# Attention scores on four 64x64 blocks of TensorE, a pair of tiles in one PSUM tile, at the start of a round

## The chip, the cores and the metric

The kernel runs on one core of a Trainium2 chip. The metric is the device time of one execution in microseconds. Engines are named as in the profile: PE (TensorE matmuls), PEld (its weight loads), DVE (VectorE), ACT (ScalarE), POOL (GpSimd), SP (the queue that issues most loads). SBUF is the on-chip memory; PSUM is the memory that matmuls write, eight banks of 2 KB in each of 128 partitions.

## What is computed

Attention within chunks of 64 positions, followed by a mixture of experts in which each token goes to one expert:

```python
# q, k, v: (8, 8, 576, 64) float32: batch, head, position, dimension
scores = matmul(q_c, k_c.T) / sqrt(64)        # in each chunk of 64 positions
attn = exp(scores - max(scores)); attn /= sum(attn) + 1e-9
x = matmul(attn, v_c)                         # -> 4608 tokens x 512 (8 heads x 64)
logits = x @ w_gate + modality_bias[modality_id]
e_idx = argmax(logits)                        # one of 8 experts
out[t] = softmax(logits)[e_idx] * (relu(x[t] @ w1[e_idx]) @ w2[e_idx])
```

All of it is float32.

## The kernel before

**Tiles.** The 4608 tokens are 36 tiles of 128 rows: two chunks of 64 positions (c = 0, 1), with all eight heads. For each tile six steps follow each other:

- `scores(t)`: 16 matmuls of 64x64x64, one for each head and chunk. Chunk c has its 64 dimensions on partitions 64c to 64c+63 of the `qk` tile, and its scores go to the same partitions of a PSUM bank `sp`. So the matmuls use two blocks of the 128x128 array by turns: rows 0-63 with columns 0-63, and rows 64-127 with columns 64-127. DVE then takes the maximum of each row of 64 (`mx`, L245) and subtracts it (`ex`, L247), 512 elements a partition each.
- `exps(t)`: the exponential on ACT (L252), and on POOL the first half of the sum (`sr`, L253). `sums(t)` on DVE finishes the sum and takes its reciprocal `ris`, which is applied later.
- `transposes(t)`: four 128x128 transposes of `ex` on PE into a bank `ap` (L264), copied by ACT to `at` (L266).
- `values(t)`: 16 matmuls of 64x64x64 on the two diagonal blocks into a bank `xp` (L278), copied by ACT to `xt` (L281).
- `rows(t)`: four matmuls over the whole array (L290), by the identity and the gate's weights, into `yb[t % 2]`: token rows (128 columns a head pair) and gate logits (16). DVE scales the rows by `ris` into `xr` (L292).
- `put(t)`: ACT copies the logits to `lp` (L302), then issues the DMA of `xr` to DRAM from its own queue (L303).

**Order.** The program is scheduled by hand: every engine runs its instructions in the order in which the code issues them. From tile 2 on, one pass of the main loop (a *round* here, a = 2, 4, ... 34) has two tiles: transposes of a; rows, sums and put of a-2, then of a-1; transposes of a+1; scores of a+2 and a+3; values of a and a+1, with the exps of a+2 ahead and those of a+3 behind. Tiles 0 and 1 go through two single-tile steps. Ahead of the loop stand scores of tiles 0 and 1 and some empty matmuls (`busy`). At the end of every tile `advance()` issues pieces of the routing (`route`, `early_table`, `late_hots`), and `plan` issues gathers, weight loads and weight splits for the last 14 tiles; these add DVE, ACT and POOL work from about a = 14 on.

**Loads.** SP issues `qk` (512 KB a tile, four buffers) right behind the scores that free the buffer, and `v` (256 KB, six buffers) behind the transposes of the round.

**PSUM.** Tag "s" has two banks (`sp`, later `hp` of the experts, and `rp`, `lt`, two of the splits), tag "t" two (`ap`, `xp`, two of the splits, `rp` of the last group, `ll`), `yb` four. A tile of a tag waits until the tile two earlier under that tag has been read.

**Experts.** `split(k)` transposes the first gathered rows (`tp`, L747) and splits them into a high part on ACT (L748) and a low part on DVE (L749). `slot(s)` runs one expert on up to 384 rows; its first layer is `first()` with `hp` (L802), its second L815 into `yb`. The first slot begins as soon as the last tiles are through. Thirteen slots follow each other, with 1248 matmuls of the first layer and 888 of the second.

Of the kernel before, what the change touches and what calls it, by code (L numbers as in the profile page):

```python
# [8 lines left out]
F32 = mybir.dt.float32  # L9
# [4 lines left out]
ALU = mybir.AluOpType  # L14
AX = mybir.AxisListType
# [80 lines left out]
def attention_moe(ctx: ExitStack, tc: tile.TileContext, qkv, mod, cst, bias, wcat, wfst, out):  # L96
# [69 lines left out]

    yb = [ps.tile([P, 2, 512], F32, name=f"yb{i}", bufs=1) for i in range(2)]

    def busy(n):
# [65 lines left out]

    def scores(t):
        b = st[t]["qk"]
        sp = ps.tile([P, H, 64], F32, tag="s", name="sp")
        for h in range(H):
            hs = slice(h * 64, h * 64 + 64)  # L240
            for c in range(2):
                cs_ = slice(c * 64, c * 64 + 64)
                PE.matmul(sp[cs_, h, :], b[cs_, 0, hs], b[cs_, 1, hs], start=True, stop=True)  # L243
        mx = wk.tile([P, H], F32, name="mx", bufs=3)
        V.reduce_max(mx, sp, axis=AX.X)  # L245
        ex = wk.tile([P, H, 64], F32, name="ex", bufs=4)
        V.tensor_tensor(ex, sp, mx.unsqueeze(2).to_broadcast([P, H, 64]), ALU.subtract)  # L247
        st[t]["ex"] = ex

# [71 lines left out]
    def route(g):  # L321
# [69 lines left out]
        ready.add(("ranks", g))  # L391
        rp = ps.tile([P, 2, 32, E], F32, tag="s" if g < NEG else "t", name="rp")
        PE.matmul(rp[:, 0, 0:n], ub, oh, start=True, stop=True)
# [78 lines left out]
    def late_whats(b0, b1):  # L472

        n = b1 - b0
        eq = wk.tile([P, H, 64], F32, name="ex", bufs=4).rearrange("p a b -> p (a b)")
        eq = eq.bitcast(BF16)[:, 0:NT * n].rearrange("p (t b) -> p t b", b=n)
        for a in range(0, NT, NT // 2):
            tp = slice(a, a + NT // 2)
            V.tensor_tensor(eq[:, tp], blkl[:, tp].unsqueeze(2).to_broadcast([P, NT // 2, n]),
                            late_to[0][:, b0:b1].unsqueeze(1).to_broadcast([P, NT // 2, n]), ALU.is_equal)  # L480
            yield
        whats.clear()
        for c in range(NT // PART):
            tp = slice(c * PART, (c + 1) * PART)
            w = wk.tile([P, DM], F32, name="v", bufs=NV).bitcast(BF16)[:, 0:PART * n * 5]
            V.tensor_tensor(
                w.rearrange("p (t b c) -> p t b c", t=PART, c=5),
                eq[:, tp].unsqueeze(3).to_broadcast([P, PART, n, 5]),
                parts[:, tp].unsqueeze(2).to_broadcast([P, PART, n, 5]), ALU.mult)
            whats.append(w.rearrange("p (t m) -> p t m", t=PART))  # L490
            for _ in range(3):
                yield
# [3 lines left out]
    def late_lists(b0, b1):  # L496

        n = b1 - b0
        assert len(whats) == NT // PART and len(late_hot) == NT
        lt = ps.tile([P, n, 5], F32, tag="t", name="ll")  # L500
        for t in range(NT):
# [15 lines left out]
    def early_table(blk, pf, oh, fm):  # L517
# [41 lines left out]
        assert "hot" in ready  # L559
        lt = ps.tile([P, NBLK, 5], F32, tag="s", name="lt")  # L560
        for t in range(n0):
# [178 lines left out]

    def split(k, tag="t"):

        hi, lo = xring[0]
        tp = ps.tile([P, 512], F32, tag=tag, name="tp")[:, 0:SLOT]
        for t in range(NTT):
# [48 lines left out]
    def first(x, w, f, n):  # L794
        hi, lo = x
        whi, wlo = w
        hp = ps.tile([P, 512], F32, tag="s", name="hp")[:, 0:n]
        m = 0
# [101 lines left out]

    scores(0)
    load_qk(NB)
    exps(0)
    late_consts()
    scores(1)
    load_qk(NB + 1)
    busy(BUSY)

    for a, n in [(0, 1), (1, 1)] + [(t, 2) for t in range(2, NT, 2)]:
        hold = transposes(a)  # L910
        if a > 1:
            for t in (a - 2, a - 1):
                rows(t)
                sums(t + 2)
                put(t)
            load_v(a + 2, hold)
            load_v(a + 3, transposes(a + 1))
            for g, (t0, m) in enumerate(GROUPS):
                if t0 + m == a:
                    jobs.append(route(g))  # L920
        else:
            if not a:
                exps(1)
            sums(a)
        small = [t for t in (range(a + 2, a + 4) if a > 1 else (a + 2,)) if t < NT]
        for t in small:
            scores(t)
            load_qk(t + NB)
        if n == 2 and small:
            exps(a + 2)  # L930
        for t in range(a, a + n):
            values(t)
            if small and (n == 1 or t > a):
                exps(small[-1])
            advance()
            plan(t - NT)
            if t >= NT - 2:
                split(t - NT + 2, "s")
        if a == 2:
            prepare()  # L940
# [29 lines left out]
def _pack(inputs):  # L970
# [5 lines left out]
    q, k, v = (chunks(np.asarray(inputs[n])) for n in ("q", "k", "v"))  # L976
    qt = q.transpose(0, 1, 4, 2, 3).reshape(NT, 2, 64, DM)
    kt = k.transpose(0, 1, 4, 2, 3).reshape(NT, 2, 64, DM)
    vv = v.reshape(NT, 2, NP, 2, 64, D).transpose(0, 3, 4, 2, 1, 5).reshape(NT, 2, 64, DM)
    qkv = np.stack([qt, kt, vv], axis=3).reshape(NT, P, 3, DM)  # L980

# [48 lines left out]
```

## Time and profile before

| | us |
|---|---|
| median of 3 runs | 563.91 (561.99 to 564.23) |
| the profiled execution's own time | 564.37 |
| its span in the profile | 562.6 |
| ACT busy | 244.8 |
| POOL busy | 185.0 |
| scores, matmuls (L243) | 38.4 |
| values, matmuls (L278) | 38.5 |

The attention stage covers about the first 137 us; after it the experts' matmuls fill PE to the end. A row of a group gives line, engine, operation, output <- input with shapes, count, busy time and mean ns of one, and behind the last bar the idle time just before and what ended it. A row of the timeline gives start and duration in us and merges equal instructions (x64). A row of a table by stretch gives the stretch, its length, and for each engine busy time and number of records, then the granted clock, the DMA share and GB/s. Matmul ends are modelled by the profiler.

### The profile page before, as it was taken

The numbers are of one execution on the slowest core, as the hardware profiler recorded it, in microseconds if no ns is written. First come the engines' busy times: TensorE is split into PE (matmuls) and PEld (weight loads), VectorE is DVE, ScalarE is ACT, GpSimd is POOL, SyncE is SP. The second block draws the span as 40 slices with busy tenths as digits, with TensorE's granted clock in tenths as the row PEclk, the third lists the DMA queues.
The fourth block names the chain that finished last, engine by engine and source line by source line (L and its number), as shares of the span: only waits on it lengthen the run. The fifth ranks groups of instructions, "written<-read, shape, count | busy, mean of one in ns | idle before, by whom it ended". The sixth has DMA issues, their size and how long they took to land.

```text
span 562.6 us, 12421 instructions
## 1 busy us (share of the span) xinstructions
PE 551.2 (98%) x4950; PEld 501.2 (89%) x4950; DVE 366.4 (65%) x645; ACT 244.8 (44%) x422; POOL 185.0 (33%) x244
## 2 busy tenths in 40 slices
PE   8999999999999999999999999999999999999995
PEld 6999898999998899999898999899899898998994
DVE  4777689788899955655656565565655656556751
ACT  3455555556444333443434434433434434435541
POOL 3322446766699933050220404013040200302011
PEclk9999999999999999999999999999999999999998
DMA  9989989899787469677574966748587673756510
GB/s 329 323 296 309 298 291 296 279 338 313 249 284 223 174 224 317 202 233 224 172 269 150 315 210 190 259 127 276 193 248 219 196 243 121 247 188 215 179 38 26
DMA packets 52754, 130.54 MB, mean 232 GB/s; under 512 B 5198, under 2 KB 22734, under 8 KB 46288
## 3 DMA queue, kind: packets, MB, share of 16 engines
q1 hardware_dynamic: 40864, 100.68, 54.9%
q0 software_dynamic: 5920, 18.88, 8.8%
q10 hardware_dynamic: 5904, 10.11, 4.9%
q8 instruction: 41, 0.67, 0.5%
q14 instruction: 25, 0.20, 0.1%
HBM read 102.12 MB, written 28.05 MB: 231 GB/s over the span
## 4 chain that ended last, share of the span: by engine, by line
issue 49%; PE 32%; POOL 9%; DVE 5%; DMA 2%; ACT 1%; POOLq 0%; ACTq 0%; DVEq 0%
PE hp L802 8%; PE yb L815 7%; PE yb L290 5%; PE sp L243 5%; POOL xg L707 5%; PE xp L278 4%; POOL out L827 3%; PE ap L264 2%; DMA qk<-in_qkv 2%; DVE wl L779 1%; PE yb L171 1%; POOL xq L432 1%; DVE ex L247 0%; DVE mx L245 0%; PE ll L502 0%
## 5 line engine op out<-in xcount | busy, mean ns | idle before, releaser
L779 DVE TENSOR_TENSOR wl<-raw,wh 128x1024 fp32r<-128x1024 f32 (+1 forms) x106 | 128.8, 1216 | 34.9 <-ACT wh L775 34.9
L805 ACT ACTIVATE hh<-hp 128x384 fp32r<-128x384 f32 (+1 forms) x104 | 49.3, 474 | 219.2 <-PE hp L802 218.9
L802 PE MATMUL hp<-xh,wh 128*128 128x384 f32 (+1 forms) x416 | 137.1, 330 | 0.0
L802 PE MATMUL hp<-xh,wl 128*128 128x384 f32 (+1 forms) x416 | 136.8, 329 | 0.0
L802 PE MATMUL hp<-xl,wh 128*128 128x384 f32 (+1 forms) x416 | 136.5, 328 | 0.2 <-DVE xl L739 0.2
L806 DVE SCALAR_TENSOR_TENSOR hl<-hp,hh 128x384 fp32r<-128x384 f32 (+1 forms) x104 | 55.6, 534 | 108.4 <-ACT hh L805 108.4
L815 PE MATMUL yb<-wh,hl 128*128 128x512 f32 x296 | 117.2, 396 | 0.0
L815 PE MATMUL yb<-wl,hh 128*128 128x512 f32 x296 | 116.5, 393 | 0.0
L815 PE MATMUL yb<-wh,hh 128*128 128x512 f32 x296 | 116.5, 393 | 0.0
L827 POOL DMA_INDIRECT out<-yo,tkl x28 | 28.0, 1002 | 248.2 <-DVE yo L826 242.7
L775 ACT CAST wh<-raw 128x1024 fp32r<-128x1024 f32 (+1 forms) x106 | 108.5, 1024 | 0.2 <-issue 0.2
L802 PEld LDWEIGHTS hp<-xl,wh 128*128 128x128 f32 x416 | 78.3, 188 | 4.7 <-DVE xl L739 0.7
L802 PEld LDWEIGHTS hp<-xh,wh 128*128 128x128 f32 x416 | 78.4, 188 | 3.8
L802 PEld LDWEIGHTS hp<-xh,wl 128*128 128x128 f32 x416 | 78.2, 188 | 0.0
L815 PEld LDWEIGHTS yb<-wh,hl 128*128 128x128 f32 x296 | 55.6, 188 | 13.4 <-DVE hl L806 0.6
L815 PEld LDWEIGHTS yb<-wh,hh 128*128 128x128 f32 x296 | 56.0, 189 | 9.1 <-ACT hh L805 0.2
L815 PEld LDWEIGHTS yb<-wl,hh 128*128 128x128 f32 x296 | 55.7, 188 | 9.1
L253 POOL TENSOR_TENSOR sr<-ex 128x256 f32<-128x256 f32 x36 | 26.4, 734 | 65.9 <-ACT ex L252 62.8
L278 PE MATMUL xp<-at,v 64*64 64x64 f32 x1152 | 38.5, 219 | 2.3 <-issue 2.2
L243 PEld LDWEIGHTS sp<-qk 64*64 64x64 f32 x1152 | 35.6, 136 | 4.2 <-DVE sm L257 2.0
L278 PEld LDWEIGHTS xp<-at,v 64*64 64x64 f32 x1152 | 36.0, 135 | 3.5 <-issue 2.9
L243 PE MATMUL sp<-qk 64*64 64x64 f32 x1152 | 38.4, 221 | 0.2 <-issue 0.2
(182 smaller groups left out, 573.9 us busy)
## 6 DMA issues: line engine op xcount, KB each, us to landing
raw<-in_wcat SPq DMA_DIRECT2D x48, 1024.0 KB, 6.2
qk<-in_qkv SPq DMA_DIRECT2D x36, 512.0 KB, 5.8
v<-in_qkv SPq DMA_DIRECT2D x36, 256.0 KB, 4.7
xd<-xr ACTq DMA_DIRECT2D x36, 256.0 KB, 4.8
xs<-xg SPq DMA_DIRECT2D x10, 768.0 KB, 7.2
xq<-xs SPq DMA_DIRECT2D x40, 192.0 KB, 3.4
raw<-in_wfst SPq DMA_DIRECT2D x4, 512.0 KB, 4.9
raw<-in_wfst SPq DMA_DIRECT2D x2, 1024.0 KB, 9.6
```

Of the source, the lines that this page charges most:

```text
L243: PE.matmul(sp[cs_, h, :], b[cs_, 0, hs], b[cs_, 1, hs], start=True, stop=True)
L253: G.tensor_tensor(sring[t % 4][:, :, 0:32], ex[:, :, 0:32], ex[:, :, 32:64], ALU.add)
L278: PE.matmul(xp[hs, p, c * 64:c * 64 + 64], v[hs, vs], at[hs, p, c * 64:c * 64 + 64], start=True, stop=True)
L290: PE.matmul(fp[:, p, 0:GWC], xt[:, p, :], gw[:, p, :], start=True, stop=True)
L707: G.indirect_dma_start(xg[:, t, :], None, xd[0:n, :], bass.IndirectOffsetOnAxis(ap=tk[:, t:t + 1], axis=0), bounds_check=n - 1, oob_is_err ...
L775: A.copy(hi, raw)
L779: (G if pool else V).tensor_tensor(lo, raw, hi.bitcast(F32), ALU.subtract)
L802: PE.matmul(hp, a[:, ks], b[:, k, 0:n], start=(m == 0), stop=(m == 3 * NK - 1))
L805: A.activation(hh[:, 0:n], hp, AF.Relu)
L806: V.scalar_tensor_tensor(hl[:, 0:n], hp, 0.0, hh.bitcast(F32)[:, 0:n], ALU.max, ALU.subtract)
L815: PE.matmul(ys[t], a[:, tsl], b[:, DM:2 * DM], start=(f == 0 and i == 0), stop=(f == NF - 1 and i == 2))
L827: w = G.indirect_dma_start(out, bass.IndirectOffsetOnAxis(ap=tk[:, t:t + 1], axis=0), yo, None, bounds_check=N - 1, oob_is_err=False)
```

## The change

The scores of two tiles are computed together. The host lays q and k out so that the two heads of a pair are on the two halves of the partitions, with both chunks beside each other. Each matmul then takes head half r (rows of the array) and chunk c (columns, and output partitions), and all four combinations occur. Half r writes bank r of a new PSUM tile `sb` of two banks, which holds both tiles of the pair. DVE takes maximum and difference of both tiles at once, 1024 elements a partition. `ex` and `mx` become pair tiles with two buffers each (only tiles 0 and 1 are still done singly, the second one in `yb[0]`).

The order of a round changes too: scores of a+2 and a+3 come first, then transposes of a; rows and sums of a-2 and a-1; transposes of a+1; both put; values of a and a+1. Tiles 0 and 1 become a round of the same form. Since `sb` takes the banks of tag "s", the other users of "s" (`hp`, the first group's `rp`, `lt`, two splits) move to tag "t", and `rp` of the last group and the late lists use the banks of `sb`.

```diff
+    sb = ps.tile([P, 2, 512], F32, name="sb", bufs=1)
...
-    def scores(t):
-        b = st[t]["qk"]
-        sp = ps.tile([P, H, 64], F32, tag="s", name="sp")
-        for h in range(H):
-            hs = slice(h * 64, h * 64 + 64)
-            for c in range(2):
-                cs_ = slice(c * 64, c * 64 + 64)
-                PE.matmul(sp[cs_, h, :], b[cs_, 0, hs], b[cs_, 1, hs], start=True, stop=True)
-        mx = wk.tile([P, H], F32, name="mx", bufs=3)
-        V.reduce_max(mx, sp, axis=AX.X)
-        ex = wk.tile([P, H, 64], F32, name="ex", bufs=4)
-        V.tensor_tensor(ex, sp, mx.unsqueeze(2).to_broadcast([P, H, 64]), ALU.subtract)
-        st[t]["ex"] = ex
+    def scores(a, its=(0, 1), to=None):
+
+        to = sb if to is None else to
+        sp = to.rearrange("q r (b k) -> q r b k", k=64)
+        w = slice(its[0] * NP, its[-1] * NP + NP)
+        for i in its:
+            b = st[a + i]["qk"]
+            for p in range(NP):
+                for r, c in ((0, 0), (1, 1), (0, 1), (1, 0)):
+                    h, o = slice(r * 64, r * 64 + 64), slice(c * 64, c * 64 + 64)
+                    ws = slice((2 * p + c) * 64, (2 * p + c) * 64 + 64)
+                    PE.matmul(sp[o, r, i * NP + p], b[h, 0, ws], b[h, 1, ws], start=True, stop=True)
+        if not its[0]:
+            st[a]["pair"] = (wk.tile([P, 2, 2 * NP], F32, name="mx", bufs=2),
+                             wk.tile([P, 2 * NP, 2, 64], F32, name="ex", bufs=2))
+        mx, ex = st[a]["pair"]
+        mx = mx[:, :, w]
+        V.reduce_max(mx, sp[:, :, w], axis=AX.X)
+        V.tensor_tensor(ex[:, w].rearrange("q a r k -> q r a k"), sp[:, :, w],
+                        mx.unsqueeze(3).to_broadcast([P, 2, len(its) * NP, 64]), ALU.subtract)
+        for i in its:
+            st[a + i]["ex"] = ex[:, i * NP:i * NP + NP].rearrange("q p r k -> q (p r) k")
...
-        rp = ps.tile([P, 2, 32, E], F32, tag="s" if g < NEG else "t", name="rp")
+        rp = ps.tile([P, 2, 32, E], F32, tag="t", name="rp") if g < NEG else \
+            sb[:, 0].rearrange("q (a n e) -> q a n e", a=2, e=E)
...
-        lt = ps.tile([P, n, 5], F32, tag="t", name="ll")
+        lt = sb[:, 1, 0:n * 5].rearrange("p (b c) -> p b c", c=5)
...
-        lt = ps.tile([P, NBLK, 5], F32, tag="s", name="lt")
+        lt = ps.tile([P, NBLK, 5], F32, tag="t", name="lt")
...
-        tp = ps.tile([P, 512], F32, tag=tag, name="tp")[:, 0:SLOT]
+        tp = ps.tile([P, 512], F32, tag="t", name="tp")[:, 0:SLOT]
...
-        hp = ps.tile([P, 512], F32, tag="s", name="hp")[:, 0:n]
+        hp = ps.tile([P, 512], F32, tag="t", name="hp")[:, 0:n]
...
-    scores(0)
+    scores(0, (0,))
     load_qk(NB)
     exps(0)
     late_consts()
-    scores(1)
+    scores(0, (1,), yb[0])
     load_qk(NB + 1)
     busy(BUSY)
-    for a, n in [(0, 1), (1, 1)] + [(t, 2) for t in range(2, NT, 2)]:
+    exps(1)
+
+    for a in range(0, NT, 2):
+        if a + 2 < NT:
+            scores(a + 2)
+            for t in (a + 2, a + 3):
+                load_qk(t + NB)
         hold = transposes(a)
-        if a > 1:
+        if a:
             for t in (a - 2, a - 1):
                 rows(t)
                 sums(t + 2)
+        else:
+            sums(0)
+            sums(1)
+        other = transposes(a + 1)
+        if a:
+            for t in (a - 2, a - 1):
                 put(t)
             load_v(a + 2, hold)
-            load_v(a + 3, transposes(a + 1))
+            load_v(a + 3, other)
...
-        small = [t for t in (range(a + 2, a + 4) if a > 1 else (a + 2,)) if t < NT]
-        for t in small:
-            scores(t)
-            load_qk(t + NB)
-        if n == 2 and small:
+        if a + 2 < NT:
             exps(a + 2)
-        for t in range(a, a + n):
+        for t in (a, a + 1):
             values(t)
-            if small and (n == 1 or t > a):
-                exps(small[-1])
+            if t > a and t + 2 < NT:
+                exps(t + 2)
             advance()
             plan(t - NT)
             if t >= NT - 2:
-                split(t - NT + 2, "s")
+                split(t - NT + 2)
```

On PE, one plain round before stood as follows (`ap`: transposes, `yb`: rows, `sp`: scores, `xp`: values):

```order
L264 MATMUL ap<-cs,ex 128x128 x4
L290 MATMUL yb_94<-cs,xt 128x144 x4
L290 MATMUL yb_95<-cs,xt 128x144 x4
L264 MATMUL ap<-cs,ex 128x128 x4
L243 MATMUL sp<-qk 64x64 x32
L278 MATMUL xp<-at,v 64x64 x32
```

The same round after the change:

```order
L248 MATMUL sb<-qk 64x64 x32
L274 MATMUL ap<-cs,ex 128x128 x4
L300 MATMUL yb_94<-cs,xt 128x144 x4
L300 MATMUL yb_95<-cs,xt 128x144 x4
L274 MATMUL ap<-cs,ex 128x128 x4
L288 MATMUL xp<-at,v 64x64 x32
```

The 32 scores matmuls moved from between the second transposes and the values to the head of the round, so the values now follow the transposes directly.

On ACT, one plain round before (`at`, `xt`: copies of transposes and values, `lp` and `xd`: the two put, `ex`: exponentials):

```order
L266 COPY at<-ap 128x512
L302 COPY lp_132<-yb_94 128x64
L303 DMA xd<-xr 128x512
L302 COPY lp_132<-yb_95 128x64
L303 DMA xd<-xr 128x512
L266 COPY at<-ap 128x512
L252 ACTIVATE ex<-ex 128x512
L281 COPY xt<-xp 128x512 x2
L252 ACTIVATE ex<-ex 128x512
```

After the change:

```order
L276 COPY at<-ap 128x512 x2
L312 COPY lp_133<-yb_94 128x64
L313 DMA xd<-xr 128x512
L312 COPY lp_133<-yb_95 128x64
L313 DMA xd<-xr 128x512
L262 ACTIVATE ex<-ex 128x512
L291 COPY xt<-xp 128x512 x2
L262 ACTIVATE ex<-ex 128x512
```

The second `at` copy moved ahead of both put; the rest kept its order, with the put directly ahead of the first exponential.

On DVE, a plain round before (`xr`: scaled rows, `sm` and `ris`: sums, `mx` and `ex`: maximum and difference of the scores):

```order
L292 TENSOR_TENSOR xr<-yb_94,ris 128x4x4x32
L257 TENSOR_REDUCE sm<-sr_137 128x8
L258 RECIPROCAL ris<-sm 128x8
L292 TENSOR_TENSOR xr<-yb_95,ris 128x4x4x32
L257 TENSOR_REDUCE sm<-sr_138 128x8
L258 RECIPROCAL ris<-sm 128x8
L245 TENSOR_REDUCE mx<-sp 128x8
L247 TENSOR_TENSOR ex<-sp,mx 128x512
L245 TENSOR_REDUCE mx<-sp 128x8
L247 TENSOR_TENSOR ex<-sp,mx 128x512
```

After the change:

```order
L254 TENSOR_REDUCE mx<-sb 128x16
L255 TENSOR_TENSOR ex<-sb,mx 128x2x8x64
L302 TENSOR_TENSOR xr<-yb_94,ris 128x4x4x32
L267 TENSOR_REDUCE sm<-sr_138 128x8
L268 RECIPROCAL ris<-sm 128x8
L302 TENSOR_TENSOR xr<-yb_95,ris 128x4x4x32
L267 TENSOR_REDUCE sm<-sr_139 128x8
L268 RECIPROCAL ris<-sm 128x8
```

Four operations on the scores became two, and they moved ahead of the rows' scaling.

More of the change, by code (lines that the diff above doesn't have):

```diff
@@ L474, in late_whats @@
         n = b1 - b0
-        eq = wk.tile([P, H, 64], F32, name="ex", bufs=4).rearrange("p a b -> p (a b)")
+        eq = wk.tile([P, 2 * NP, 2, 64], F32, name="ex", bufs=2).rearrange("p a r b -> p (a r b)")
         eq = eq.bitcast(BF16)[:, 0:NT * n].rearrange("p (t b) -> p t b", b=n)
@@ L739, in part, with split @@
         V.tensor_tensor(l, x, h.bitcast(F32), ALU.subtract)
-    def split(k, tag="t"):
+    def split(k):
         hi, lo = xring[0]
-        tp = ps.tile([P, 512], F32, tag=tag, name="tp")[:, 0:SLOT]
+        tp = ps.tile([P, 512], F32, tag="t", name="tp")[:, 0:SLOT]
         for t in range(NTT):
@@ L920, in attention_moe @@
                     jobs.append(route(g))
[L921 to L924, printed above, removed]
-        small = [t for t in (range(a + 2, a + 4) if a > 1 else (a + 2,)) if t < NT]
-        for t in small:
-            scores(t)
-            load_qk(t + NB)
-        if n == 2 and small:
+        if a + 2 < NT:
             exps(a + 2)
-        for t in range(a, a + n):
+        for t in (a, a + 1):
             values(t)
-            if small and (n == 1 or t > a):
-                exps(small[-1])
+            if t > a and t + 2 < NT:
+                exps(t + 2)
             advance()
@@ L976, in _pack @@
     q, k, v = (chunks(np.asarray(inputs[n])) for n in ("q", "k", "v"))
[L977 to L980, printed above, removed]
+    q, k, v = (a.reshape(NT, 2, NP, 2, 64, D) for a in (q, k, v))
+    qt = q.transpose(0, 3, 5, 2, 1, 4).reshape(NT, P, DM)
+    kt = k.transpose(0, 3, 5, 2, 1, 4).reshape(NT, P, DM)
+    vv = v.transpose(0, 3, 4, 2, 1, 5).reshape(NT, P, DM)
+    qkv = np.stack([qt, kt, vv], axis=2)
     wg = np.asarray(inputs["moe_w_gate"])
```

## The prediction

> **What bounds the kernel now.** I read the page first, then busy times by stretch, then one round of the timeline.
>
> ```profile
> PE 551.2 (98%) x4950; PEld 501.2 (89%) x4950; DVE 366.4 (65%) x645; ACT 244.8 (44%) x422; POOL 185.0 (33%) x244
> ...
> L243 PE MATMUL sp<-qk 64*64 64x64 f32 x1152 | 38.4, 221 | 0.2 <-issue 0.2
> ```
>
> PE is busy for 98% of the span, so time goes where PE's own stream gets shorter, as long as nothing else closes the gap. The change touches the scores (L243), 38.4 us of PE, all of it in the attention stage. That stage is a chain of rounds of two tiles. Seven rounds run from 21.80 to 71.42, and eight more to 129.20:
>
> ```profile
> core 0: us, PE busy (x) PEld busy (x) DVE busy (x) ACT busy (x) POOL busy (x), PEclk, DMA share, GB/s
> 21.80:71.42 49.62, 48.65 (x1066) 46.71 (x1064) 35.47 (x72) 26.08 (x56) 16.55 (x22) 1.00 0.89 297
> 71.42:129.20 57.78, 56.27 (x1234) 53.88 (x1232) 49.67 (x130) 30.77 (x68) 36.79 (x77) 1.00 0.89 301
> ```
>
> PE is without work for only 1.0 of 49.6 and 1.5 of 57.8 us. DVE has 5.07 us a round in the first stretch and 6.21 in the second, where the routing work is added; the clock is full. One plain round, in the timeline (start, duration):
>
> ```profile
> 49.51 0.66 PE L264 MATMUL ap<-cs,ex 128*128 128x128 f32 x4
> 50.00 2.13 PE L290 MATMUL yb<-cs,xt 128*128 128x144 f32 x16
> ...
> 51.24 0.69 DVE L292 TENSOR_TENSOR xr<-yb,ris 128x512 f32<-128x512 f32 x1 [1.68 <-ACT at L266]
> ...
> 51.96 0.60 PE L264 MATMUL ap<-cs,ex 128*128 128x128 f32 x4
> ...
> 52.42 0.68 DVE L292 TENSOR_TENSOR xr<-yb,ris 128x512 f32<-128x512 f32 x1
> ...
> 52.49 2.08 PE L243 MATMUL sp<-qk 64*64 64x64 f32 x64
> ...
> 53.13 0.21 ACT L302 COPY lp<-yb 128x64 f32<-128x64 f32 x1 [0.96 <-DVE xr L292]
> 53.14 0.64 ACTq L303 DMA_DIRECT2D xd<-xr  x1
> ...
> 53.69 0.69 DVE L245 TENSOR_REDUCE mx<-sp 128x8 f32<-128x512 f32 x1
> 53.88 0.58 ACT L266 COPY at<-ap 128x512 f32<-128x512 f32 x1 [0.53 <-PE sp L243]
> ...
> 54.41 2.03 PE L278 MATMUL xp<-at,v 64*64 64x64 f32 x64
> ...
> 55.20 0.63 ACT L252 ACTIVATE ex<-ex 128x512 f32<-128x512 f32 x1 [0.74 <-DVE ex L247]
> 55.73 0.57 ACT L281 COPY xt<-xp 128x512 f32<-128x512 f32 x1
> ...
> 56.37 0.66 PE L264 MATMUL ap<-cs,ex 128*128 128x128 f32 x4
> ```
>
> From start to start PE spends 0.49 (transposes), 1.96 (rows), 0.53 (transposes), 1.92 (scores) and 1.96 (values): 6.86 us, and nothing else fits between.
>
> **The scores: half, or nothing.** Two tiles are 32 matmuls, and the trace has 64 records for them, two passes each. With 0.22 for the last record, 64 start within 1.86 us: 58 ns a matmul, 29 a pass. A pass of the rows streams 144 columns in 1.96/16 = 0.1225 us, 0.85 ns a column, so 64 columns take some 54 ns. Passes that start 29 ns apart therefore already run two at a time, one on each diagonal block, and each block is full. The change keeps 32 matmuls and 64 passes but gives each of four blocks a quarter of them. No row shows two blocks that share rows or columns of the array. The bounds are 32 x 58/2 = 0.93 us (all four overlap) and 1.87 (the added two take turns with the old). How PE runs past a matmul that waits is seen where its instructions ran out within the values (records in flight in each stretch):
>
> ```profile
> 20.42:20.46 0.04, 0.04 (x4) 1.00 0.26 102
> 20.48:20.52 0.04, 0.04 (x2) 1.00 1.13 410
> 20.53:20.57 0.04, 0.04 (x1) 1.00 2.66 563
> 20.59:21.07 0.48, 0.00 (x0) 1.00 0.86 286
> 61.60:61.62 0.02, 0.02 (x8) 1.00 0.55 205
> 61.63:61.67 0.04, 0.04 (x6) 1.00 0.95 359
> 61.69:61.73 0.04, 0.04 (x4) 1.00 1.05 410
> ```
>
> At 61.6 the stock drains in twos, 8, 6, 4. At 20.4 it drains 4, 2, 1, 0: two single passes, some 55 ns apart, a last matmul alone on its block. In the program both passes of a matmul stand together. If passes began strictly in that order, a second pass would pair with the next matmul's first, and one single pass would be left at the end, not two. So PE starts the other block's matmul ahead of a second pass that waits. That speaks for a bookkeeping by block, and I take 0.93; the end 1.87 stays in the range.
>
> [...]
>
> **DVE.** Four operations of 512 elements (0.69 each, 2.76 us) become two of 1024. The nearest row of that size:
>
> ```profile
> L779 DVE TENSOR_TENSOR wl<-raw,wh 128x1024 fp32r<-128x1024 f32 x102 | 125.7, 1233 | 34.9 <-ACT wh L775 34.9
> ```
>
> That is 2 x 1.23 = 2.46, so 0.3 us less a round. But they now stand ahead of the two xr.
>
> **The new order closes part of the gap.** Count from a round's first scores matmul with 0.98 us for the scores. Alone, PE would be at the next round's scores at 6.86 - 0.94 = 5.92 and at its first transposes at 6.90. These wait for the copy xt(a), since xp and ap share two banks. On ACT xt(a) is behind both lp copies, both DMA issues and one exp. The scores' last pass ends at 1.13; the reduce starts at 1.18 (0.05 later, as at 53.69 behind its own tile), xr(a-2) at 1.18 + 2.46 = 3.64, xr(a-1) 1.18 later (51.24 to 52.42) and ends at 5.50; lp at 5.53; lp to the next ACT work is 0.75 (53.13 to 53.88), so exp at 6.28, xt 0.53 later at 6.81, done at 7.38, seen by PE at 7.45. With the first issue's length (0.33 in place of 0.64) it is 7.13. So the transposes wait 0.23 to 0.55, and from them to the following scores PE needs 0.49 + 1.96 + 0.53 + 1.96 = 4.94. Two rounds take 7.29 + 4.94 = 12.2, one **6.1 us**: 0.76 saved, not 0.94. The copy at(a+1), which was covered by the scores, is now covered by values(a): transposes end about 0.6 after their start, the copy takes 0.58, and values(a+1) come 0.53 + 0.98 after that start, 0.3 to spare.
>
> Seven plain rounds give 7 x 0.76 = 5.3 us. In the other eight DVE has 1.14 us a round more. A plain round leaves DVE free for about 1.3 us before the next reduce, but the extra is uneven:
>
> ```profile
> 85.46:92.69 7.23, 7.20 (x153) 6.83 (x153) 6.81 (x22) 3.58 (x8) 4.57 (x13) 1.00 0.85 279
> 100.87:108.00 7.13, 6.94 (x156) 6.63 (x152) 5.21 (x12) 3.75 (x9) 5.43 (x14) 1.00 0.69 238
> 115.47:122.34 6.87, 6.87 (x157) 6.64 (x153) 5.39 (x15) 3.78 (x9) 3.49 (x5) 1.00 1.04 407
> ```
>
> In the first of these it overflows by half a microsecond, in the second not; POOL's 5.43 and the third's 407 GB/s leave little too. I take 0.5 a round, 4.0 us, between 0.3 and 0.65.
>
> **Two edits that cost.** Splits and hp now draw from the two "t" banks, in the order xp(34), tp, xp(35), tp, tp, tp, hp.
>
> ```profile
> 133.65 0.59 ACT L281 COPY xt<-xp 128x512 f32<-128x512 f32 x1
> ...
> 133.81 1.15 PE L278 MATMUL xp<-at,v 64*64 64x64 f32 x32
> ...
> 136.78 0.86 ACT L748 CAST xh<-tp 128x384 fp32r<-128x384 f32 x2 [0.77 <-PE tp L747]
> ...
> 136.83 0.42 PE L802 MATMUL hp<-xh,wh 128*128 128x384 f32 x1
> ...
> 137.31 1.01 DVE L749 TENSOR_TENSOR xl<-tp,xh 128x384 fp32r<-128x384 f32 x2
> ```
>
> The last values now wait for the copy at 133.65 to end (134.24, not 133.81: 0.45). The first hp waits until DVE has read the third tp, half of 1.01 after 137.31: 137.8 and not 136.83, 1.0. The tp in between wait some 0.3. Sum 1.8 us; nothing hides it, as PE has no other work there. It could be 1 if DVE gets there earlier.
>
> At the start the second pair's scores move ahead of the first transposes and need the fourth qk, which tile 3 used at 11.87 before:
>
> ```profile
> 6.69 8.12 SPq L116 DMA_DIRECT2D qk<-in_qkv  x4
> 8.41 0.66 PE L264 MATMUL ap<-cs,ex 128*128 128x128 f32 x4 [0.28 <-ACT ex L252]
> 11.87 1.15 PE L243 MATMUL sp<-qk 64*64 64x64 f32 x32
> ```
> ```profile
> SPq L116 <- DMA qk<-in_qkv: 3.1, 1, 3.1
> ```
> ```profile
> qk<-in_qkv SPq DMA_DIRECT2D x12, 512.0 KB, 5.4
> ```
>
> After the issue at 6.69 SP waited 3.1 us for the landing of that load, to about 10.1, and then issued the sixth. So the first transposes slip from 8.41 to some 10.8; copy and two values bring PE to 14.2, where the third pair needs the sixth qk (10.2 + 5.4 at the latest, so 14.8 to 15.6); its transposes follow at 15.3 to 16.1 and the next round's 4.94 + 0.98 later, at 21.2 to 22.0, where they were at 21.80. I take 0, within half a microsecond either way. SP's later loads keep two rounds' lead for qk and one for v. The other tile moves (rp, lt, late lists) go to banks that nobody holds then; I cost them at nothing, under 0.3 each if one waits.
>
> **Sum**, against the profiled execution (span 562.6, time 564.37): -5.3 - 4.0 + 1.8 + 0 = -7.5, so 556.9. That execution lies 0.46 above the median of 563.91, so the forecast is **556.4** beside the median. Its own bounds: 0.94 and 0.65 a round with a tail of 1 give 553; 0.6 and 0.3 with the full tail give 560.
>
> **Rivals.**
> - *The added blocks overlap only partly, or the rounds close on transfers.* At 1.4 us a pair PE's round is 6.39: 0.47 x 7 + 0.35 x 8 - 1.8 = 4.3 saved, 560. A round moves 297 GB/s x 7.09 us = 2.1 MB, which in 6.1 us is 345 GB/s. The row with 407 speaks against a hard stop, the share of 0.89 at 297 for later loads and for more time lost where instructions run out. 558 to 563.
> - *The added blocks take turns* (strict order, or one queue for each half of the rows). Rounds stay at 6.86, and tail and start are paid: 564 + 1.8 + 0.3, about 566. The 54 ns that a block's pass needs anyway allow it; the drain speaks against strict order, not against a queue by rows.
> - *Slower: a weight load no longer hides when the block changes within the same rows.* Then each matmul pays one pass more on its half of the rows, 3 x 58 in place of 2 x 58, and 16 a half take 2.8 us in place of 1.87: 17 rounds x 0.93 + 1.8 give 581. It shows as a loss once a matmul costs over 60 ns, since the tail's 1.8 us then has company. For it: no row has such a change of block. Against it: the loads of a block already hide under its own passes (some 55 ns a pass in the drain). [...]
>
> **Chances.** Forecast 0.56, partly or transfers 0.16, turns 0.22, exposed loads 0.06. A change under 0.5% (2.8 us) is about what a measurement cannot tell from none. Faster: nearly all of the first and over half of the second, 0.64. Same: the rest of the second and most of the third, 0.24. Slower: a quarter of the third and the last, 0.12. The range 552 to 566.5 takes in the first three but for their ends.
>
> **What would show it.** The 64 score records of a pair within 1.2 us and not 2.1; rounds near 6.1 where they were 6.86; a short idle of PE ahead of each first transposes, put down to xt; DVE operations of 1.2 us on sb; the first hp about 1 us behind its last tp. If the scores last 2.1 us again, the forecast is wrong at its first step; if they shrink and rounds don't, the chain through DVE and ACT was read wrongly.

## The result, and the profile after

The kernel became slower: 567.43 us (median of 8 runs, 564.93 to 568.27) beside 562.48 for the kernel before on the same chip. The ratio is 1.0077, with a 95% interval of 1.0054 to 1.0099; one of the eight executions of the kernel before took 908.99 us and is not in it. The profiled execution took 567.57 us, its span is 565.8 (before: 564.37 and 562.6). Times below are from the span's start; *gap* means the time from one start of a PE instruction to the next.

The page's first line:

```profile
PE 539.6 (95%) x4950; PEld 487.0 (86%) x4950; DVE 362.4 (64%) x611; ACT 243.5 (43%) x422; POOL 185.1 (33%) x244
```

PE has 11.6 us less to do than before (551.2), and yet the span is 3.2 us longer: PE now stands still for 26 us, where it was 11. A plain round in the timeline, PE and the two operations of DVE on `sb` alone:

```profile
52.12 0.66 PE L274 MATMUL ap<-cs,ex 128*128 128x128 f32 x4
52.17 1.22 DVE L254 TENSOR_REDUCE mx<-sb 128x16 f32<-128x1024 f32 x1 [1.05 <-PE sb L248]
...
52.61 2.13 PE L300 MATMUL yb<-cs,xt 128*128 128x144 f32 x16
...
53.50 1.22 DVE L255 TENSOR_TENSOR ex<-sb,mx 128x1024 f32<-128x1024 f32 x1
...
54.57 0.60 PE L274 MATMUL ap<-cs,ex 128*128 128x128 f32 x4
...
55.10 2.02 PE L288 MATMUL xp<-at,v 64*64 64x64 f32 x62
...
56.91 0.27 PE L248 MATMUL sb<-qk 64*64 64x64 f32 x2
56.96 0.23 PE L288 MATMUL xp<-at,v 64*64 64x64 f32 x2
57.02 1.10 PE L248 MATMUL sb<-qk 64*64 64x64 f32 x62
...
58.06 0.33 PE L274 MATMUL ap<-cs,ex 128*128 128x128 f32 x1
```

The scores last 1.1 us (2.08 before), so all four blocks work at once; DVE's two operations take 1.22 us each; and this round takes 58.06 - 52.12 = 5.94 us. But few rounds are like it. From the first transposes of tile 4 to those of tile 34 (15 rounds), and in two short stretches:

```profile
24.84:130.47 105.63, 92.87 (x2238) 87.61 (x2233) 82.86 (x171) 54.69 (x123) 53.67 (x99) 0.98 0.88 298
18.00:20.00 2.00, 2.00 (x10) 2.00 (x10) 1.89 (x3) 0.51 (x1) 0.00 (x0) 0.50 0.95 346
120.00:122.00 2.00, 2.00 (x42) 2.00 (x43) 0.86 (x3) 0.29 (x2) 0.72 (x1) 0.55 1.04 405
```

Fifteen rounds of 5.94 would be 89; they take 105.6, with PE idle for 12.8 us. At the start (17.8 to 21.2 us) and behind a long wait (120.2 to 123.6) its clock was down to half; the last two rows lie there. The five largest of PE's waits from 24.84 to 130.47 (engine, line, releaser; total, times, longest):

```profile
PE sb L248 <- issue: 4.0, 4, 2.2
PE xp L288 <- DMA v<-in_qkv: 2.6, 1, 2.6
PE ap L274 <- ACT xt L291: 2.3, 4, 1.0
PE yb L300 <- issue: 1.4, 1, 1.4
PE rp L404 <- DMA v<-in_qkv: 0.9, 1, 0.9
```

"issue" is idle time without any wait. The largest such place in the timeline:

```profile
35.85 1.09 PE L248 MATMUL sb<-qk 64*64 64x64 f32 x56
39.10 0.34 PE L248 MATMUL sb<-qk 64*64 64x64 f32 x6 [2.16 <-issue]
```

Six score records are left when PE stops for 2.2 us, and neither semaphore nor buffer holds them. Counting PE's instructions in the trace gives the reason. Among the DMA records there are 41 packets of 16 KB on the queue that the page calls "q8 instruction". Beside the six gaps of over 0.3 us without a wait between 24.84 and 130.47 they read (columns: start and length of the packet; number of the instruction behind the gap, with PE's first as number 0; the gap; from the packet's end to PE's next start):

```
36.77 0.88 | no. 1473 = 193 +  5 x 256 | gap 2.38 | 1.46
43.24 0.95 | no. 1729 = 193 +  6 x 256 | gap 0.77 | 1.27
59.59 0.96 | no. 2497 = 193 +  9 x 256 | gap 0.38 | 1.39
65.56 0.96 | no. 2753 = 193 + 10 x 256 | gap 1.69 | 1.31
70.50 1.01 | no. 3009 = 193 + 11 x 256 | gap 1.18 | 1.31
104.42 0.96| no. 4545 = 193 + 17 x 256 | gap 0.58 | 1.36
```

Every gap lies ahead of an instruction 256 n + 193, and ends 1.3 to 1.5 us after a packet: PE's program arrives in **blocks of 256 instructions**, and these blocks came late. In the rounds here a packet began 0.6 to 4.1 us after PE had begun the block before it, that is, less than one block ahead.

Three losses remain, at the start, in the late rounds and at the end of the stage:

```profile
10.31 0.69 PE L248 MATMUL sb<-qk 64*64 64x64 f32 x32 [1.17 <-DMA qk<-in_qkv]
10.94 1.09 PE L274 MATMUL ap<-cs,ex 128*128 128x128 f32 x8
...
16.61 0.69 PE L248 MATMUL sb<-qk 64*64 64x64 f32 x32 [1.35 <-DMA qk<-in_qkv]
17.24 0.66 PE L274 MATMUL ap<-cs,ex 128*128 128x128 f32 x4
17.73 3.80 PE L300 MATMUL yb<-cs,xt 128*128 128x144 f32 x16
```
```profile
85.54 0.21 ACT L312 COPY lp<-yb 128x64 f32<-128x64 f32 x1 [0.96 <-DVE xr L302]
...
85.92 0.63 ACT L262 ACTIVATE ex<-ex 128x512 f32<-128x512 f32 x1 [0.17 <-issue]
...
86.45 1.05 ACT L291 COPY xt<-xp 128x512 f32<-128x512 f32 x2
...
87.07 0.65 PE L274 MATMUL ap<-cs,ex 128*128 128x128 f32 x4 [0.60 <-ACT xt L291]
```
```profile
119.96 3.42 PE L288 MATMUL xp<-at,v 64*64 64x64 f32 x62 [2.60 <-DMA v<-in_qkv]
```
```profile
135.29 1.15 PE L288 MATMUL xp<-at,v 64*64 64x64 f32 x32 [0.21 <-ACT xt L291]
136.78 0.55 PE L758 MATMUL tp<-cs,xg 128*128 128x128 f32 x3 [0.34 <-DVE xl L760]
...
139.80 0.44 PE L813 MATMUL hp<-xh,wh 128*128 128x384 f32 x1 [0.76 <-DVE xl L760]
```

At the start, scores wait twice for their loads, and the rows at 17.73 then run at the clock of 0.50 seen above (3.5 us between their first and last start, not 1.84). In the late rounds the chain xr, lp, exp, xt ends 0.6 us after PE is ready. The values of tile 30 wait 2.6 us for `v` and run at half clock behind that wait. At the end the splits share two banks. The ledger of the two profiled executions, which lie 3.2 us apart (the two medians some 5), in us:

| | before | after | |
|---|---|---|---|
| first transposes of tile 4 | 21.80 | 24.84 | +3.0 |
| from there to those of tile 34 | 107.40 | 105.63 | -1.8 |
| from there to the first hp | 7.6 | 9.3 | +1.7 |
| the experts | 425.8 | 426.0 | +0.2 |

### The profile page after: what moved, and what is told of

It is laid out like the page before. It is cut to its first block, busy times and chain, and to the rows that moved or that the text cites. A ratio compares the mean times of both kernels' runs of the same rounds, so it can differ in the third digit from the quotient of the medians.

```text
span 565.8 us, 12373 instructions
## 1 busy us (share of the span) xinstructions
PE 539.6 (95%) x4950; PEld 487.0 (86%) x4950; DVE 362.4 (64%) x611; ACT 243.5 (43%) x422; POOL 185.1 (33%) x244
## 3 DMA queue, kind: packets, MB, share of 16 engines
q1 hardware_dynamic: 40864, 100.68, 54.9%
## 4 chain that ended last, share of the span: by engine, by line
issue 49%; PE 29%; POOL 8%; DMA 6%; DVE 5%; ACT 1%; SPq 0%; POOLq 0%; ACTq 0%; DVEq 0%
PE hp L813 8%; PE yb L826 7%; POOL xg L718 5%; PE yb L300 4%; PE xp L288 4%; DMA qk<-in_qkv 4%; POOL out L838 3%; DMA v<-in_qkv 3%; PE ap L274 2%; PE sb L248 2%; DVE xr L302 1%; DVE wl L790 1%; DVE mx L254 0%; PE sb L513 0%; DVE xq L744 0%
## 5 line engine op out<-in xcount | busy, mean ns | idle before, releaser
L288 PEld LDWEIGHTS xp<-at,v 64*64 64x64 f32 x1152 | 36.7, 139 | 7.2 <-issue 3.0
L300 PE MATMUL yb<-cs,xt 128*128 128x144 f32 x288 | 40.3, 294 | 1.4 <-issue 1.4
L300 PEld LDWEIGHTS yb<-cs,xt 128*128 128x128 f32 x288 | 38.2, 197 | 1.5 <-issue 1.5
```

The source lines that it names most:

```text
L288: PE.matmul(xp[hs, p, c * 64:c * 64 + 64], v[hs, vs], at[hs, p, c * 64:c * 64 + 64], start=True, stop=True)
L300: PE.matmul(fp[:, p, 0:GWC], xt[:, p, :], gw[:, p, :], start=True, stop=True)
```

## The experiments

Two theories stood against each other. **Deliveries**: PE now asks for loads and instructions faster than the transfers bring them, so what its own work saves comes back as gaps and waits. **PE and its chain**: the rounds are as long as PE's work and the chain through DVE and ACT; the gaps are an accident or belong to the new blocks. The table has what was measured; ratios are against runs of the kernel before on the same chip, with their 95% intervals, and *gaps* sums the gaps over 0.3 us without a wait between tiles 4 and 34. The times themselves come from several chips: beside e1 to e4 the kernel before had a median of 564.10, beside e5 to e8 562.28, beside e9 and e10 563.88, beside e11 and e12 564.09. The columns from "tile 4 at" on are of one profiled execution each.

| run | us (runs) | ratio | tile 4 at | 4 to 18 | 18 to 34 | gaps |
|---|---|---|---|---|---|---|
| before | 562.48 (8) | | 21.80 | 49.6 | 57.8 | 2.6 |
| changed | 567.43 (8) | 1.0077 (1.0054-1.0099) | 24.84 | 48.4 | 57.3 | 7.0 |
| e1 again | 566.35 (1) | | 24.78 | 46.9 | 57.3 | 5.0 |
| e2 diagonal | 569.97 (4) | 1.0108 (1.0042-1.0175) | 24.50 | 48.2 | 59.0 | 2.0 |
| e3 old place | 594.77 (4) | 1.0542 (1.0481-1.0602) | 21.98 | 55.8 | 75.3 | 0 |
| e4 start, tail | 564.20 (10) | 1.0003 (0.9968-1.0039) | 22.08 | 50.1 | 57.7 | 10.0 |
| e5 few loads | 564.12 (1) | | 24.74 | 44.0 | 57.0 | 1.9 |
| e6 shift | 566.45 (1) | | 23.56 | 48.1 | 56.6 | 6.2 |
| e7 put later | 561.92 (10) | 0.9995 (0.9968-1.0022) | 23.17 | 48.8 | 52.6 | 8.3 |
| e8 all mends | 562.89 (12) | 1.0004 (0.9983-1.0025) | 21.92 | 49.1 | 54.9 | 12.1 |
| e9 loads apart | 560.67 (10) | 0.9937 (0.9913-0.9961) | 22.03 | 47.6 | 53.2 | 9.9 |
| e10 v one round | 560.93 (12) | 0.9956 (0.9928-0.9984) | 22.12 | 49.2 | 54.6 | 8.0 |
| e11 diagonal | 564.54 (12) | 1.0014 (0.9999-1.0030) | 23.73 | 48.8 | 54.3 | 0 |
| e12 no v | 553.61 (1) | | 22.35 | 42.8 | 51.8 | 1.9 |

In the traces of all these kernels there are 67 such gaps; all 67 lie at the beginning of a block (in e12 the count is one less, as a missing record makes it), and PE started again 1.2 to 1.6 us after the packet's end. Seven more, of 0.5 to 1.1 us, lie at the beginning of a block and end as close behind a packet, but their instruction has a wait as well, so they are not in the sums; with them e4 comes to 10.8, e8 to 14.0, e9 to 10.4, e10 to 9.0, e11 to 0.5 and e12 to 2.8.

**e1: the changed kernel again**, with no edit.

> The changed kernel once more. Theory A (supply): PE's instructions come in blocks of 256, and where the next block's packet is late PE stands still at the block's first instruction, with nothing that it waits for. In the trace at hand 7.0 us are lost so between 24 and 130 us. A expects gaps of 0.3 to 2.4 us again, 4 to 10 us in all, all at the first instruction of a block, each ending 1.2 to 1.5 us after the end of a 16 KB packet; the blocks that are late may be others. Rival: chance of that one execution; then under 3 us in all. The waits for xt in the rounds with much DVE work (0.8 to 1.2 us) and the one for v (2.8 us) should be at the same places by either.

The larger gaps were at the same instructions: 2.27, 0.77 and 1.61 us at 36.6, 44.4 and 65.5, as were the waits for xt, rp and v. The late blocks are a property of the program and not of one execution; the small gaps at 61.6 and 106.2 were not there, and the one near 71 was 0.35 us and not 1.18.

**e6: shifted by 64 instructions.**

```diff
+    for _ in range(32):
+        PE.matmul(yb[1][:, 1, 0:64], warm[:, 0:P], warm[:, 0:64], start=True, stop=True)
     busy(BUSY)
     exps(1)
```

> The changed kernel with 32 small empty matmuls (64 instructions) more at the start, where PE waits for q and k anyway. Supply theory: the blocks of 256 now end 64 instructions earlier in the work, so the gaps move to other places of the rounds (no longer 36.6, 44.4, 65.5 us, at scores, scores, rows), are again all at the first instruction of a block, and sum up to 4 to 9 us between tiles 4 and 34; the time stays within 2 us of the changed kernel. Rival: the gaps belong to places in the work (scores that share rows); then they stay at the same scores.

The gaps went to 29.2, 36.2, 57.4, 63.0, 69.7 and 98.2, at other instructions of the work but again at numbers 256 n + 193, 6.2 us in all. So the place follows the block, not the work. That five of six still fall in scores fits too: there a block is used up fastest (in the changed kernel's round above the 64 records of the scores start within 0.99 us, those of the values within 1.86). Besides, the stretch 18 to 20 ran at full clock here, and tile 4 came 1.3 us earlier. That the extra matmuls did it is not shown: e2 and e7, which lack them, kept the full clock there too.

```profile
18.00:20.00 2.00, 2.00 (x18) 1.89 (x17) 1.89 (x3) 0.35 (x1) 0.00 (x0) 1.00 1.00 377
```

**e2: the new order, scores on the diagonal blocks.**

```diff
-                for r, c in ((0, 0), (1, 1), (0, 1), (1, 0)):
-                    h, o = slice(r * 64, r * 64 + 64), slice(c * 64, c * 64 + 64)
-                    ws = slice((2 * p + c) * 64, (2 * p + c) * 64 + 64)
-                    PE.matmul(sp[o, r, i * NP + p], b[h, 0, ws], b[h, 1, ws], start=True, stop=True)
+                for r in range(2):
+                    hs = slice((2 * p + r) * 64, (2 * p + r) * 64 + 64)
+                    for c in range(2):
+                        o = slice(c * 64, c * 64 + 64)
+                        PE.matmul(sp[o, r, i * NP + p], b[o, 0, hs], b[o, 1, hs], start=True, stop=True)
```

> Order, pair tile and banks of the changed kernel, but the scores on the two diagonal blocks as before (host layout as before). Rival (PE bound in every round): the scores take 1.87 us a pair again, and all of 17 x 0.93 = 15.8 us comes on top: 583. Theory A and the chain: a round without a stall lasts 6.9 us, but a block of 256 instructions then lasts about 5.8 us as before and not 5.0, so the gaps without a wait shrink from 7 us to 2 to 4; the waits for xt (4 us over the late rounds) vanish, since PE comes there 0.9 us later. So 15.8 - 4 - 4 = some 8 us on top: 573 to 577. The late start (first transposes of tile 4 at 24.8 and not 21.8) stays.

570, less than either reading gave: four blocks, which take 15.8 us off PE's work, bring 0.3% by the two ratios in this order, some 2 us, and as the two intervals overlap, no gain at all is shown. From tile 4 to 18 PE has 0.93 us a round more to do, and the seven rounds take 48.2 us, as in the changed kernel (48.4), with no gap in place of 6.4 us of them.

**e5: without the loads of some tiles.** `load_qk` for tiles 12 to 21 and `load_v` for 8 to 17 issue nothing; these tiles work on older data.

> The changed kernel without the loads of q and k of tiles 12 to 21 and of v of tiles 8 to 17: these tiles work on what lies in the buffers from earlier tiles (so the output and the routing differ; only the stretch up to tile 20 is read). The loads that are left out would be issued in the rounds a = 6 to 14. Supply theory with DMA load: the 16 KB packets come late because they queue among those loads. Then from a = 8 to 18 the packets come at most 1.5 us after the block before began, no gap without a wait is left there (5 to 7 us in the changed kernel between tiles 4 and 18), and a round lasts 5.95 to 6.0 us. Rival: a packet takes its 2.5 to 4 us whatever else moves; then the gaps stay at 4 to 6 us. Second rival: blocks of 64x64 on the same rows stall PE by themselves; then the gaps stay and their ends have nothing to do with packets.

The same stretch in the changed kernel, then without those loads, and what PE waited for in e5 from 36 to 66:

```profile
36.40:63.50 27.10, 24.19 (x593) 22.76 (x587) 18.96 (x32) 14.07 (x33) 5.76 (x8) 1.00 0.91 309
```
```profile
36.61:63.68 27.07, 26.59 (x639) 25.45 (x635) 21.18 (x34) 15.87 (x36) 8.42 (x11) 1.00 0.29 98
```
```profile
PE ap L281 <- ACT xt L298: 0.4, 1, 0.4
```

Packets came 0.5 to 1.2 us after the block before began, and the four rounds from 36.9 to 61.2 took 6.44, 5.93, 6.04 and 5.93 us. One gap, 1.47 us, came at 67.0, when the loads had started again (its packet began 2.3 us into the block). So the same instructions on the same blocks run without a gap when fewer bytes move: the packets are late because of the other transfers. That falsifies the readings in which shared rows stall PE, or a packet always takes its 2.5 to 4 us.

**e4: start and splits mended.** The first rounds in the order of before, and `tp` in `sb`:

```diff
-        tp = ps.tile([P, 512], F32, tag="t", name="tp")[:, 0:SLOT]
+        tp = sb[:, k % 2, 0:SLOT]
...
+    for a in (0, 1):
+        transposes(a)
...
+        scores(2, (a,))
+        load_qk(a + 2 + NB)
+        values(a)
```

> The changed kernel with two mends: the first rounds in the order of before (tiles 2 and 3 by single tiles, scores of 4 and 5 behind the transposes of 3; the new order from a = 4 on), and the splits' tp in the banks of sb, which are free by then. If start and tail cost what the traces say, first transposes of tile 4 at 21.5 to 22.5 (was 24.84) and transposes of 34 to the first hp 7.6 us (was 9.3): 3 + 1.7 less, 562 to 564. Rival: PE is held by deliveries (instructions, qk, v) and gets no further: what the start gains comes back as gaps and waits up to 130 us, and only the tail's 1.7 is left, 565.7.

The start's 2.8 us were won. In the profiled execution 2.2 of them were lost again by tile 34: the gaps had grown from 7 to 10 us, and the clock stood at 0.50 from 70.9 to 77.7, behind a gap of 3.0 us. But this execution (568.08) lies 4 us above its own median, so it does not show what the others kept: by the ratios the time is 0.7%, some 4 us, below the changed kernel's. The splits did not gain: 10.0 us in place of 9.3, since the third and fourth `tp` now wait for DVE to read the first two.

**e3: four blocks in the old place**, tile by tile: the main loop of before, with `scores(t - t % 2, (t % 2,))`.

> Scores on four blocks, but where they stood before: in the round between transposes of a+1 and values, tile by tile, with the start of the kernel before; banks and tail as in the changed kernel. Start: first transposes of tile 4 at 20.5 to 21.5 us. A round: DVE still has xr, sm, xr, sm ahead of the first reduce, so ex of a+2 is ready 5.6 us after the round's first transposes, exp 0.7 later: the next transposes come after 6.4 us, not 6.86 and not 5.93. 15 x 0.46 = 6.9 saved against before, less some 2 us more of gaps without a wait; the tail costs 1.7. So 558 to 561. If only PE's work counted (rounds of 5.93), 551 to 554; if the four blocks themselves are what costs (gaps as large as in the changed kernel), 563 to 566.

```profile
PE sb L248 <- DVE ex L255: 29.8, 15, 3.0
```

A miss of the edit's own making: with one `sb` for both tiles, the second tile's scores wait 2.0 us for DVE to read the first, in every round. It says nothing on the place.

**e7: put later**, behind the first copy xt of the round:

```diff
-            for t in (a - 2, a - 1):
-                put(t)
             load_v(a + 2, hold)
...
             values(t)
+            if t == a and a:
+                put(a - 2)
+                put(a - 1)
```

> The changed kernel with put (logits copy, issue of the rows' DMA) moved on ACT behind the first copy xt of the round, so that neither exp nor that copy stands behind xr on DVE. The chain: the waits of the first transposes on xt in the late rounds (0.8, 1.2, 0.8, 0.9, 1.2 to 1.4 us) go, PE gains 3 to 4 us there, 563 to 565. Rival: deliveries hold the stage, the gain comes back as gaps without a wait or a longer wait for v: within 1.5 us of the changed kernel's 567.

All of PE's waits from tile 4 to 34:

```profile
PE sb L248 <- issue: 5.2, 3, 1.9
PE yb L300 <- issue: 1.8, 2, 1.1
PE xp L288 <- DMA v<-in_qkv: 1.2, 2, 0.8
PE xp L288 <- ACT xt L291: 0.2, 1, 0.2
```

The waits of the transposes on xt (gaps of 0.4 to 1.2 us, 4.3 in all in the changed kernel) are gone, the late rounds take 4.7 us less, and the time falls by 0.8%, to that of the kernel before. So the chain was a cause; but the loss for `v` shrank too (2.8 to 1.5 us, and no half clock behind it), so not all of the 4.7 us is the chain's. Another 1.7 us came at the start, where the clock stayed full this time; it fell to half from 37.4 to 40.8, behind a gap of 2.1 us. The gaps rose by 1.3 us.

**e8: all mends.** Start of e4, put of e7; the first two `tp` in `sb`, the other two in "t", the first `hp` in `sb`; and `load_v` two rounds ahead.

> Four mends together: start in the order of before; splits' tp in the two banks of sb for the first two and tag t for the others, first hp in sb; put later as in the run before this; v loaded two rounds ahead in place of one. If each gives what its wait cost: start 2.7, tail 1.7, xt 3.5, v 2.6 and 1.3 for the clock behind it: 11.8 off 567.4, 555.6. Supply theory: what the start and the rounds gain comes back in part as gaps at the beginnings of blocks (in the run with start and tail alone 10 us of them): 558 to 562. If everything but the tail is given back: 564 to 566.

From tile 4 to 34:

```profile
21.92:125.90 103.98, 92.40 (x2232) 86.70 (x2232) 82.56 (x171) 54.90 (x125) 54.17 (x100) 1.00 0.94 327
```

Deliveries at their clearest: the waits for xt and v are down to 0.2 and 1.0 us and the clock is full, but 12.1 us of gaps have taken their place. The tail, from the transposes of 34 to the first `hp`, took 8.6 us, 0.7 less than in the changed kernel. Against the changed kernel e4 alone brought 0.7%, e7 alone 0.8%, and all four mends together 0.7%: the sum of the single waits (555.6) was far off.

**e9 and e10: loads apart.** On e8, SP's four loads of a round follow four different points of PE's work in place of two:

```diff
             scores(a + 2)
-            for t in (a + 2, a + 3):
-                load_qk(t + NB)
+            load_qk(a + 2 + NB)
...
+        mid_ = rows(a - 2)
...
+            load_v(t, mid_)
...
+            load_qk(a + 3 + NB, other)
...
+            mid_ = values(t)
+            if t == a:
+                load_v(a + 4 + 1, mid_)
```

Here `rows` and `values` return their last matmul and `other` is the last transpose of a+1; each load waits for the one it is given. In e10 `load_v` is one round ahead.

> All mends, and SP's four loads of a round no longer in one row (q,k; q,k; v; v within 3 us) but apart: first q,k behind the scores, first v behind the rows of a-2, second q,k behind the transposes of a+1, second v behind the values of a. In the trace of the changed kernel the late 16 KB packets come just as SP's queue of loads has run empty (at 31.0 and 36.8 us), once a round. If the packet waits behind what that queue holds, it now comes at most 2.5 us after the block before began, the gaps at block beginnings fall from 12 us between tiles 4 and 34 to under 4, and the time to 554 to 558. Rival: the bytes themselves are the bound (2.1 MB a round at 340 GB/s are 6.2 us), packets stay late: gaps over 7 us, 560 to 563.

> The same with v one round ahead as in the changed kernel in place of two. If v two rounds ahead is needed, values wait for v near tile 30 again (1 to 4 us) and the time is that much above the run before; if spreading alone brings v in time, within 1 us of it, or up to 1.5 us better, since two loads of v less lie in the first rounds.

e9 is the fastest version: 0.6% below the kernel before. But not for the reason given. Packets came 3.2 us on average into the block before (3.1 in e8), not under 2.5, and 9.9 us of gaps stayed; my reading that a packet waits until SP's queue is empty found no support. What gained the 3.2 us on e8 between tiles 4 and 34 is not shown; the share of the transfers rose from 0.94 to 0.96:

```profile
22.03:122.83 100.80, 92.59 (x2233) 87.09 (x2233) 82.36 (x171) 55.00 (x125) 53.33 (x98) 1.00 0.96 328
```

A share of 0.96 over 100 us leaves little to win. In e10 the values waited for v again (gaps of 1.7 and 1.8 us near 115), yet its time lies within e9's interval.

**e11 and e12: the two sides of e9.** e11 puts the scores on the diagonal blocks again (the edit of e2); e12 leaves out the loads of `v` for tiles 8 to 33, which work on older data.

> The fastest version so far (all mends, loads apart) with the scores on the two diagonal blocks again (host layout as before): all else equal, what are the four blocks worth? If PE bounds the rounds, 0.93 us for each of 17 pairs comes on top of 560.7: 576. If deliveries (loads and instructions) bound them, the gaps at block beginnings (9.9 us there) and waits shrink by most of it: a round is at least 6.9 us of PE work, 15 of them 103 to 105 us in place of 100.8, the gaps under 3 us, the time 562 to 566.

> The fastest version without the loads of v of tiles 8 to 33 (they work on the v that lies in the buffers; output and routing differ, read only up to the transposes of tile 34): a quarter less loads a round, all else equal. If the bytes bound the rounds, tiles 4 to 34 take 92 to 96 us and not 100.8, and the gaps at block beginnings are under 4 us and not 9.9. If the packets are late whatever moves, or the chain through DVE and ACT bounds the rounds, 98 to 101 us.

e11 and e12, from tile 4 to 34:

```profile
23.73:126.81 103.08, 102.66 (x2237) 98.46 (x2233) 81.96 (x171) 53.83 (x122) 52.95 (x99) 1.00 0.94 313
```
```profile
22.35:116.98 94.63, 91.42 (x2233) 86.42 (x2233) 82.86 (x172) 55.53 (x126) 53.71 (x100) 1.00 0.84 281
```

With the diagonal blocks PE is busy for all but 0.4 us, no gap without a wait is left, and the fifteen rounds take 103.1: PE is the bound. With four blocks PE's work falls to 92.6, the transfers stand at 0.96, and the rounds take 100.8. With the loads of `v` gone, a fifth of the bytes (281 GB/s over 94.6 us in place of 328 over 100.8), they take 94.6, most of them 5.9 to 6.2 us, with gaps of 1.9. So in the mended order four blocks are worth 0.8% (0.9937 against 1.0014, 4.3 us) where PE's own saving is 15.8. In the fifteen rounds they bring 2.3 us with all loads and 8.5 without most of `v`, of 14 that PE saves there: the transfers take the larger part.

## Why the prediction was wrong

- **Scores 1.87 to 0.93 a pair: right**, with luck: the drain it rested on had blocks of different rows only. 62 records start within 0.88 us, four every 58 ns. Nor do the records start strictly in program order, by which the added two blocks might have taken turns with the old: in the rows at 56.91 to 57.02 two score records start ahead of the last two of the values (56.91 and 56.92 us beside 56.96 and 56.97), which stand earlier in the program.
- **DVE's 2 x 1.23 and the chain to xt: right in kind.** Undisturbed rounds take 5.9 to 6.0, a little under the 6.1: the forecast had PE wait 0.23 to 0.55 us for xt in every plain round, and up to tile 18 it never did. In the late rounds the chain costs 0.4 to 1.2 us, and in e7 these waits went when the put moved out of it.
- **Tail +1.8: right**, 1.7, at the three places named.
- **Start "0, within half a microsecond": wrong by 3.0.** The first transposes came at 10.94 (forecast 10.8), but the sixth `qk` landed at 16.57 and not by 15.6, and the stretch behind it took 7.6 us and not 5.92, since the clock fell to half after PE's waits. The forecast priced waits, and not a clock of 0.50 behind them, as from 17.8 to 21.2 us. That waits bring it is not shown: with similar waits e2, e6 and e7 kept the full clock, and tile 4 still came at 23.2 to 24.5.
- **Rounds 5.3 + 4.0 us: the step that failed.** They brought 1.3 + 0.5. In the sum the round's chain was taken as the only alternative to PE's own work; the third resource stood in the quoted rows. The share of 0.89 over a round of 7.09 us is 6.3 us of transfers, which already exceeds the forecast round. I turned the same row into 345 GB/s and set one row of 407 GB/s against it; that row holds for a stretch that moves a different mix, and at a share of 1.04. As for where it went: fifteen undisturbed rounds of 5.94 are 89.1 us, and these losses make up the rest to 105.6 within 0.6: gaps of blocks 7.0, xt 4.3, v 2.8 and the clock behind it some 1.5, rp 1.0, lt 0.5. The forecast (107.4 - 9.3 = 98.1) had left room for 9 of these 17, for xt alone.
- **The rival "rounds close on transfers" was the right mechanism** with too small a price (558 to 563) and too small a chance (0.16). It was priced without the losses at the start and the tail growing alongside, and the quoted idle of 20.42 to 21.07 in the kernel before, read there only for its order of blocks, was already a late block (number 705 = 193 + 2 x 256).

What stays open: how the 16 KB packet is served among the other transfers. That it comes early when they are few is shown (e5); neither the length of SP's queue nor its spacing explained when it comes (e9). Whether the bytes or the number of the transfers count was not tried apart, as e5 and e12 leave out both. Whether e8 without v two rounds ahead, and with loads as they were, would have reached e7's time was not tried.

## What to carry to other kernels

Before shortening the busiest engine's work, multiply the share of the next resource by the length of a round: 0.89 x 7.09 = 6.3 us of transfers was near a floor here, and an engine at 98% hid it; no version with all its loads came below 6.7 us a round on average. Instructions are a transfer too, 41 packets of 16 KB for PE here: with 308 PE instructions in a round of 5.94 us a block of 256 lasts 4.9 us on average, where it was 5.7 before, and idle time at a fixed spacing of instruction numbers, put down to "issue", was that in all 67 gaps. Mending single waits of this stage moved the loss elsewhere: in e8 those for xt and v fell to 0.2 and 1.0 us, and the gaps rose from 7.0 to 12.1. In a stage that deliveries bound, try the removal of the load itself first, as in e5 or e12, to see what is to be had at all.

## What the hardware showed unexpectedly

- 67 gaps, all at instructions 256 n + 193 of PE, ending 1.2 to 1.6 us after the end of a 16 KB packet that itself lasts 0.9 to 1.9 us.
- Four 64x64 blocks of fp32 matmuls started in step, four passes every 58 ns, those that share rows included (62 records within 0.88 us); the first two records of the scores overtook the last two of the values before them (56.91 beside 56.96 us).
- The granted clock fell to half, for 3.4 us in all these cases but e4 (6.8 us): after PE stood still for 2.8 us in the changed kernel (from 120.2), for 2.1 in e7 (37.4), for 3.0 in e4 (70.9), and near 17 us (17.8 in the changed kernel), after six gaps of 0.4 to 1.6 us from 5 us on, in all three traces of the same start (changed, e1, e5). It stayed full after a gap of 2.4 us at 36.7 in the changed kernel, after one of 3.6 us at 115.4 in e6, and after similar gaps at the start of e2, e6 and e7. So the length of a gap alone does not decide it; what does is not shown.
